# One accumulation instead of two: the other row half's carried products in a recurrent-attention kernel

## The chip, the cores and the metric

The kernel runs on one core of a Trainium2 chip. The core has a matrix engine (TensorE; PE in the rows below, with PEld for its weight loads), a vector engine (DVE), a scalar engine (ACT), a general engine (POOL) and a queue that issues transfers (SP). Matmul results land in eight accumulator banks of 128 rows by 512 words; only PE, DVE and ACT reach them. The metric is the device time of one execution in microseconds (us), lower is better.

## The reference

Two parts follow each other, over 4 sequences of 768 positions.

```python
# part 1, for 8 heads of 40: a gated outer-product memory
m_new = np.maximum(f[t] + m, i[t])
C = exp(f[t] + m - m_new) * C + exp(i[t] - m_new) * outer(v[t], k[t])
n = exp(f[t] + m - m_new) * n + exp(i[t] - m_new) * k[t]
y[t] = sigmoid(o[t]) * (C @ q[t]) / maximum(abs(n @ q[t]), 1.0)
# part 2, for 4 experts of 64 on x = y: causal softmax attention of each
# expert, of which the two with the largest gate logits are summed
out = sum over the two of w[e] * (softmax(causal(q_e @ k_e.T / 8)) @ v_e @ wo[e])
```

## The kernel before

Part 1 works through 24 chunks of 128 positions (4 sequences of 6; they are numbered 0 to 23 through all sequences here), each of two sub-chunks of 64 positions. A chunk's output is the sum of two products: the *intra* products (scores inside a sub-chunk times values) and the *carried* products (queries times the state that the sub-chunk begins with). The first four chunks take another way ("narrow"); the other 20 are what the change is about.

For these 20, TensorE is used as tiles of 64 rows by 64 columns. The 8 heads lie in two row halves, and two matmuls on different row halves run side by side if they write different banks. The intra products of head parity a come from row half a and go to bank `py[a]`. The carried products of heads 0 to 3 come from row half 0 and those of heads 4 to 7 from row half 1. So half of the carried products have the row half of the bank that they belong to, here called the *same half*, and the rest have the other one, the *cross* products. Before, the same half is added to `py` by the matmuls themselves, while the cross products go to two spare banks `pi`, are copied by ACT to a tile `pc`, and DVE adds `pc` to `py`. After that ACT takes the absolute value of each head's denominator (tile `two`), DVE reduces it (`den`), multiplies with the output gate and the reciprocal, and the result `xt` is turned by PE (matmuls `one<-cst,xt`) for part 2.

All matmul results are views of one ring of eight banks, called `one`. In the rows below `one<-nat,dm` are the intra products of a chunk, `one<-sts,qs` its carried products, `one<-kqs` the scores of the next chunk, `one<-nat,ks` the next chunk's state increments. Part 2's projections are `one<-xh,WH`, `one<-WH,xh` and the like, its scores `one<-KH,QH`, its transposes `one<-cst,A`, its mixing `one<-AT,V`. A trace counts each of these 4-byte matmuls twice (two passes).

The order of the work is written as strings of steps (`UNIT`: S is a chunk's output, I the scores of the next, C its increments, L a load, P its decay tables, X the transposes, and small letters are part 2). A planner (`Tape.plan`) records all instructions, keeps matmuls in groups, and sets each engine's order by costs that it assumes; it may take up to twelve groups ahead if the first one would wait. So an edit in one step can move instructions of every engine. All instructions are emitted at one line, L618.

Of the kernel before, what the change touches and what calls it, by code (L numbers as in the profile page):

```python
# [19 lines left out]
HALF = S // 2  # L20
D1 = D + 1
T = P // 2
# [47 lines left out]
    "f45 m43 s46 f46 r45 p7,1 r44 m44 r46 s47 f47 r47 m45 m46 m47 p7,0 p7,2"  # L70
)
FIRST = (
    "S0 I0 C0 L0 P0 q0 X0 S1 I1 C1 L1 P1 k0 v2 X1 S2 I2 C2 L2 P2 g q1 k1 X2"
)
UNIT = (
    "m0 S0 I0 C0 L0 v0 v1 X0 P0 f0 s0 f1 s1 S1 I1 C1 L1 m1 k0 q0 p0 p1 p2 X1 f2 s2 s3 f3 P1 S2 I2 C2 q1 "
    "k1 v2 g P2 f4 f5 s4 s5 L2 X2"
)
PENULT = (
# [556 lines left out]
def mlstm_moe_kernel(ctx, tc, kq, nat, ig, fg, wqkv, wo, const, out):  # L636
# [3 lines left out]
    nc = tape = Tape(tc.nc)  # L640
# [5 lines left out]
    def buf(tag, shape, dtype=F32):  # L646
        return View(Buf(rings[tag], shape, dtype))
# [67 lines left out]
    eG = keep("eG", [P, NPE * H], F32)  # L715
# [7 lines left out]
    def dm_from_pe(b, j):  # L723
        return b == 0 and j < NPE

    def narrow(b, j):

        return b * NCH + j < NARROW
# [392 lines left out]
        state[b] = sprev  # L1121
        p1st[(b, j, "i")] = (nt, qc, dm, sin)

    def carried(b, j, out, pairs, start=False, stop=False):

        _, qc, _, sin = p1st[(b, j, "i")]
        for g in range(2):
            for k, zas in enumerate(pairs):
                for sub in range(j == 0, 2):
                    for z, a in zas:  # L1130
                        nc.tensor.matmul(
                            out(z, a)[rows[sub], g * D1 : (g + 1) * D1],
                            qc[heads[z], 2 * g + a, rows[sub]],
                            sin[sub][heads[z], 2 * g + a, :],
                            start=start and g == k == 0,
                            stop=stop and g == 1 and zas is pairs[-1],
                        )

    def sums(b, j):

        nm = f"{b}_{j}"
        py = [one(f"py_{nm}_{a}") for a in range(2)]
        pe = dm_from_pe(b, j)
        nt, _, dm, _ = p1st[(b, j, "i")]
        tape.cut(True)
        for c in range(4):
            for sub in range(2):
                for r, p in zip(rows, py):
                    nc.tensor.matmul(
                        p[rows[sub], c * D1 : (c + 1) * D1],  # L1150
                        dm[r, c, sub, :],
                        nt[r, (sub * 4 + c) * D1 : (sub * 4 + c + 1) * D1],
                        start=c == 0,
                        stop=c == 3 and (pe or j == 0 and sub == 0),
                    )
        tape.cut()
        pyv = [p[:, : 4 * D1].rearrange("p (c d) -> p c d", d=D1) for p in py]
        if not pe:
            pi = [one(f"pi_{nm}_{z}") for z in range(2)]
            tape.cut(True)  # L1160
            carried(b, j, lambda z, a: pi[z], (((0, 1), (1, 0)),), True, True)
            carried(b, j, lambda z, a: py[a][:, 2 * z * D1 :], (((0, 0), (1, 1)),), stop=True)
            tape.cut()
            r = slice(T if j == 0 else 0, P)
            pc = buf("pc", [P, 2, 2 * D1], F32)
            for z in range(2):
                nc.scalar.activation(pc[r, z], pi[z][r, : 2 * D1], AF.Copy)
                y = py[1 - z][r, 2 * z * D1 : 2 * (z + 1) * D1]
                nc.vector.tensor_tensor(y, y, pc[r, z], op=ALU.add)
        else:  # L1170
            pi = [one(f"pi_{nm}_{z}") for z in range(2)]
            tape.cut(True)
            carried(b, j, lambda z, a: pi[z][:, 2 * a * D1 :], (((0, 0), (1, 0)), ((0, 1), (1, 1))), True, True)
            tape.cut()
            r = slice(T if j == 0 else 0, P)
            n = P - r.start
            pc = buf("facb", [P, 2, 2, 2, D1], F32)
            for z in range(2):
                nc.vector.tensor_tensor(
                    pc[r, z],  # L1180
                    pi[z][r, : 4 * D1].rearrange("p (a g d) -> p a g d", a=2, g=2),
                    eG[r, j * H + 4 * z : j * H + 4 * z + 4]
                    .rearrange("p (g a) -> p a g", g=2)[:, :, :, None]
                    .to_broadcast([n, 2, 2, D1]),
                    op=ALU.mult,
                )
            for a in range(2):
                y = py[a][r, : 4 * D1].rearrange("p (z g d) -> p z g d", z=2, g=2)
                nc.vector.tensor_tensor(y, y, pc[r, :, a], op=ALU.add)
        p1st.pop((b, j, "i"))  # L1190
        return pyv

    def p1_state(b, j):
        nt = p1st[(b, j, "i")][0]
        o_n = nt[:, 2 * NV + DM :] if narrow(b, j) else nt[:, NKV:NNAT]
        xf = buf("xt", [P, 3 * P], F32)
        eo = xf[:, 0:DM].rearrange("p (h d) -> p h d", d=D)
        nc.scalar.activation(xf[:, 0:DM], o_n, AF.Tanh, scale=0.5)
        if narrow(b, j):
            parts = [(sums_narrow(b, j), slice(0, H))]  # L1200
        else:
            parts = [(y, slice(a, H, 2)) for a, y in enumerate(sums(b, j))]
        den = buf("den", [P, H], F32)
        twos = two[(b * NCH + j) % len(two)]
        for y, hs in parts:
            nc.scalar.activation(twos[:, hs, 0], y[:, :, D], AF.Abs, scale=2.0)
        nc.vector.tensor_reduce(den, twos, axis=AX.X, op=ALU.max)
        dens = den[:, :, None].to_broadcast([P, H, D])
        if b * NCH + j < EX:
            for y, hs in parts:  # L1210
                nc.vector.scalar_tensor_tensor(y[:, :, 0:D], eo[:, hs], 1.0, y[:, :, 0:D], op0=ALU.add, op1=ALU.mult)
            nc.vector.reciprocal(den, den)
            for y, hs in parts:
                nc.vector.tensor_tensor(eo[:, hs], y[:, :, 0:D], dens[:, hs], op=ALU.mult)
        else:
            for y, hs in parts:
                nc.vector.scalar_tensor_tensor(eo[:, hs], eo[:, hs], 1.0, y[:, :, 0:D], op0=ALU.add, op1=ALU.mult)
            nc.vector.reciprocal(den, den)
            tape.either(eo, eo, dens, op=ALU.mult)
        nc.scalar.activation(xf[:, DM : 3 * P], xf[:, 2 * P : DM], AF.Copy)  # L1220
        p1st[(b, j, "x")] = xf
# [442 lines left out]
    def run(text, k):  # L1664

        for f in text.split():
            a = int(f[1:] or 0)
            n = 3 * k + SH + a
            if f[0] == "S" and 3 <= n - 1 < NC:
                p1_state(*chunks[n - 1])  # L1670
            elif f[0] == "I" and n < NC:
                p1_intra(*chunks[n])
            elif f[0] == "C" and n < NC:
# [91 lines left out]
```

## Time and profile before

| what | us |
|---|---|
| median of three runs | 292.54 |
| the three runs | 292.54, 294.46, 291.70 |
| span of the profiled execution | 291.4 |

The profiled execution is known by its span, from its first to its last instruction; that is 0.3 us under the fastest of the three runs and 1.1 us under their median. Times in the rows are us from the start of that span. A matmul's end is modelled, and matmuls overlap, so the distance between two starts tells more than one matmul's length.

### The profile page before, as it was taken

Reading aid. Unit: us, or ns where it says so; the run is one execution under the profiler, and the core shown is the slowest. Engines: PE = TensorE matmul, PEld = TensorE weight load, DVE = VectorE, ACT = ScalarE, POOL = GpSimd, SP = SyncE. Lnnn points to the kernel's source line nnn. Section 1 sums busy time; section 2 is a strip of 40 time slices with the busy share of each in tenths; the row PEclk is TensorE's granted clock in tenths of the full one; section 3 lists DMA queues with packets and bytes.
Section 4 is the critical chain, followed back from the end, with each engine's and each line's share of the span. In section 5 each row is a group of like instructions: output and inputs, shape, how many; then the busy total and the mean of one; then the engine's idle time right before and its main releaser. Section 6 shows DMA issues by size and latency. Waiting matters only on the chain.

```text
span 291.4 us, 12993 instructions
## 1 busy us (share of the span) xinstructions
PE 279.5 (96%) x5128; PEld 242.2 (83%) x5128; DVE 220.7 (76%) x852; ACT 213.8 (73%) x714; POOL 166.5 (57%) x284
## 2 busy tenths in 40 slices
PE   8988999869999999999999999999999999999994
PEld 3876898759889978799889978798989976987884
DVE  7679387847896897657886888577878895588983
ACT  8983459829895887657895887567876895597971
POOL 3678298858889556958587628955870341014000
PEclk9999999979999999999999999999999999999999
DMA  7989769983566455645453537625401000100101
GB/s 217 293 262 282 188 178 236 251 188 110 130 194 184 116 157 167 172 124 169 137 173 112 170 100 200 196 95 146 133 6 71 2 0 2 71 3 0 70 26 45
DMA packets 31580, 39.18 MB, mean 134 GB/s; under 512 B 2784, under 2 KB 25280, under 8 KB 31520
## 3 DMA queue, kind: packets, MB, share of 16 engines
q1 hardware_dynamic: 31472, 38.26, 45.9%
q8 instruction: 40, 0.66, 0.9%
q14 instruction: 20, 0.16, 0.2%
q10 hardware_dynamic: 48, 0.10, 0.1%
HBM read 34.22 MB, written 4.13 MB: 132 GB/s over the span
## 4 chain that ended last, share of the span: by engine, by line
PE 74%; DVE 8%; ACT 5%; issue 4%; DMA 4%; POOL 3%; SPq 1%; DVEq 0%; ACTq 0%; POOLq 0%
PE one L618 74%; DMA nat<-in_nat 4%; ACT dm L618 2%; DVE A L618 2%; POOL qs L618 1%; SPq L618 1%; DVE one L618 1%; DVE sts L618 1%; ACT A L618 1%; POOL yl L618 1%; ACT AT L618 1%; DVE dm L618 0%; DVE facb L618 0%; POOL xt L618 0%; DVE xt L618 0%
## 5 line engine op out<-in xcount | busy, mean ns | idle before, releaser
L618 ACT ACTIVATE A<-A,nmx 128x128 f32<-128x128 f32 (+5 forms) x96 | 64.0, 671 | 3.7 <-DVE nmx L618 3.5
L618 DVE CUSTOM_DVE_ANT_0 A<-one,maskw 128x384 f32<-128x384 f32 (+4 forms) x96 | 45.0, 495 | 0.4
L618 ACT ACTIVATE AT<-one 128x256 f32<-128x256 f32 (+3 forms) x96 | 35.5, 428 | 6.3 <-PE one L618 6.1
L618 PE MATMUL one<-AT,V 128*64 128x384 f32 (+2 forms) x360 | 39.8, 370 | 0.0
L618 PE MATMUL one<-xl,WH 128*128 128x384 f32 x96 | 33.2, 346 | 2.3 <-issue 2.3
L618 PE MATMUL one<-xh,WH 128*128 128x384 f32 x96 | 34.7, 361 | 0.5 <-DVE xt L618 0.5
L618 PEld LDWEIGHTS one<-AT,V 128*64 128x64 f32 x360 | 22.5, 137 | 14.9 <-issue 11.6
L618 POOL TENSOR_TENSOR qs<-kqs,eqs 112x512 f32<-112x512 f32 x20 | 26.2, 1311 | 10.8 <-PE one L618 10.5
L618 PE MATMUL one<-cst,A 64*128 64x64 f32 x672 | 31.6, 226 | 0.0
L618 PEld LDWEIGHTS one<-cst,A 64*128 64x128 f32 x672 | 27.5, 138 | 2.9 <-issue 0.6
L618 POOL TENSOR_TENSOR dm<-dm,cst 128x512 f32<-128x512 f32 x20 | 25.7, 1286 | 6.3 <-DMA dm<-gd 5.0
L618 PE MATMUL one<-KH,QH 64*128 64x384 f32 (+4 forms) x128 | 27.2, 375 | 0.0
L618 POOL TENSOR_TENSOR ks<-nat,dm 128x320 f32<-128x320 f32 x24 | 17.8, 743 | 14.5 <-ACT dm L618 6.9
L618 PE MATMUL one<-KL,QH 64*128 64x384 f32 (+4 forms) x128 | 23.9, 319 | 0.0
L618 PE MATMUL one<-KH,QL 64*128 64x384 f32 (+4 forms) x128 | 23.8, 319 | 0.0
L618 DVE COPY AT<-one 128x384 f32<-128x384 f32 (+3 forms) x48 | 21.0, 456 | 2.5 <-PE one L618 2.2
L618 PEld LDWEIGHTS one<-xh,WH 128*128 128x128 f32 x96 | 18.5, 193 | 4.6 <-issue 3.4
L618 ACT ACTIVATE xh<-one 128x192 fp32r<-128x192 f32 (+1 forms) x45 | 13.0, 335 | 12.3 <-PE one L618 12.2
L618 PE MATMUL one<-xh,WL 128*128 128x384 f32 x64 | 22.0, 343 | 0.0
L618 PE MATMUL one<-WH,xh 128*128 128x260 f32 x72 | 21.5, 301 | 0.0
L618 DVE TENSOR_TENSOR dm<-one,dm 128x256 f32<-128x256 f32 (+1 forms) x44 | 18.7, 440 | 3.3 <-POOL ks L618 3.1
L618 DVE CUSTOM_DVE_ANT_0 A<-one,maskw,nmx 128x320 f32<-128x320 f32 (+1 forms) x32 | 18.5, 579 | 2.8 <-DVE nmx L618 1.0
(143 smaller groups left out, 812.9 us busy)
## 6 DMA issues: line engine op xcount, KB each, us to landing
kqs<-in_kq SPq DMA_DIRECT2D x24, 448.0 KB, 5.6
nat<-in_nat SPq DMA_DIRECT2D x20, 484.0 KB, 5.7
dm<-gd SPq DMA_DIRECT2D x40, 128.0 KB, 3.7
eqs<-ge SPq DMA_DIRECT2D x40, 96.0 KB, 5.3
out<-ob SPq DMA_DIRECT2D x24, 160.0 KB, 1.9
nat<-in_nat SPq DMA_DIRECT2D x4, 320.0 KB, 6.4
A<-in_wqkv SPq DMA_DIRECT2D x3, 386.0 KB, 6.8
nat<-in_nat SPq DMA_DIRECT2D x8, 82.0 KB, 6.3
```

What stands on the lines that cost most here:

```text
L618: f(*[fix(x) for x in op.a], **{k: fix(v) for k, v in op.k.items()})
```

## The change

The cross products are no longer given banks of their own. `sums` now issues the intra products and the same half in one group and returns; a new step N (`p1_rest`), which stands behind I and C, issues the cross products into `py` itself and then the rest of the denominators. Between the two, ACT takes those denominators of `py[1]` that are complete already (the second half of its heads). With this the denominators take three ACT instructions instead of two. The copies to `pc`, the additions and the banks `pi` are left for chunk 23 alone, which has no next chunk. A branch for chunks that compute their decay table on PE, which no wide chunk took, goes as well.

```diff
 UNIT = (
-    "m0 S0 I0 C0 L0 v0 v1 X0 P0 f0 s0 f1 s1 S1 I1 C1 L1 m1 k0 q0 p0 p1 p2 X1 f2 s2 s3 f3 P1 S2 I2 C2 q1 "
+    "m0 S0 I0 C0 N0 L0 v0 v1 X0 P0 f0 s0 f1 s1 S1 I1 C1 N1 L1 m1 k0 q0 p0 p1 p2 X1 f2 s2 s3 f3 P1 S2 I2 C2 N2 q1 "
...
+        carried(b, j, lambda z, a: py[a][:, 2 * z * D1 :], ((0, 0), (1, 1)), stop=True)
         tape.cut()
...
+        if later:
+            return by_head(py)
+        pi = [one(f"pi_{nm}_{z}") for z in range(2)]
+        tape.cut(True)
+        carried(b, j, lambda z, a: pi[z], ((0, 1), (1, 0)), True, True)
+        tape.cut()
...
+        if not narrow(b, j) and later:
+            nc.scalar.activation(twos(b, j)[:, H // 2 + 1 :: 2, 0], parts[1][0][:, 2:4, D], AF.Abs, scale=2.0)
+            p1st[(b, j, "s")] = xf, parts
+            return
...
+    def p1_rest(b, j):
+
+        if (b, j, "s") not in p1st:
+            return
+        xf, parts = p1st.pop((b, j, "s"))
+        tape.cut(True)
+        carried(b, j, lambda z, a: parts[a][0][:, 2 * z : 2 * z + 2, :].rearrange("p c d -> p (c d)"), ((0, 1), (1, 0)), stop=True, skip_group_check=True)
+        tape.cut()
+        p1st.pop((b, j, "i"))
+        nc.scalar.activation(twos(b, j)[:, 0:H:2, 0], parts[0][0][:, :, D], AF.Abs, scale=2.0)
+        nc.scalar.activation(twos(b, j)[:, 1 : H // 2 : 2, 0], parts[1][0][:, 0:2, D], AF.Abs, scale=2.0)
+        finish(b, j, xf, parts)
...
-                p1_state(*chunks[n - 1])
+                p1_state(*chunks[n - 1], n < NC)
+            elif f[0] == "N" and 3 <= n - 1 < NC:
+                p1_rest(*chunks[n - 1])
```

On PE, at chunk 14 (about 140 us in the trace), the first two rows of each kind stand in this order before; the number behind `one` is the bank, and the first carried pair writes the spare banks 65 and 70, the second the banks 68 and 67 of the intra products:

```order
L618 MATMUL one_68<-nat_157,dm_82 64x41
L618 MATMUL one_67<-nat_157,dm_82 64x41
...
L618 MATMUL one_65<-sts_162,qs_85 64x41
L618 MATMUL one_70<-sts_162,qs_85 64x41
...
L618 MATMUL one_68<-sts_162,qs_85 64x41
L618 MATMUL one_67<-sts_162,qs_85 64x41
...
L618 MATMUL one_66<-kqs_148 64x64
L618 MATMUL one_64<-kqs_148 64x64
...
L618 MATMUL one_69<-nat_155,ks_154 64x41
L618 MATMUL one_63<-nat_155,ks_154 64x41
...
L618 MATMUL one_65<-WH_172,xh_91 128x260
```

And now, on the same engine at the same chunk:

```order
L618 MATMUL one_70<-nat_157,dm_82 64x41
L618 MATMUL one_64<-nat_157,dm_82 64x41
...
L618 MATMUL one_70<-sts_162,qs_85 64x41
L618 MATMUL one_64<-sts_162,qs_85 64x41
...
L618 MATMUL one_63<-kqs_148 64x64
L618 MATMUL one_65<-kqs_148 64x64
...
L618 MATMUL one_66<-nat_155,ks_154 64x41
L618 MATMUL one_67<-nat_155,ks_154 64x41
...
L618 MATMUL one_64<-sts_162,qs_85 64x41
L618 MATMUL one_70<-sts_162,qs_85 64x41
...
L618 MATMUL one_68<-WH_172,xh_91 128x260
```

Eight of the sixteen carried matmuls moved behind the next chunk's scores and increments and write the intra products' banks 64 and 70; the number of matmuls is the same.

On ACT, at chunk 14, the order before was (`A` is an exponential of part 2, `dm` that of a decay table, `xt<-nat` the output gate's tanh, `yh` a copy of part 2):

```order
L618 ACTIVATE A_77,zs_107<-A_77,nmx_129 128x384
L618 ACTIVATE pc_86<-one_65 128x82
L618 ACTIVATE pc_86<-one_70 128x82
L618 ACTIVATE A_76,zs_107<-A_76,nmx_128 128x256
L618 ACTIVATE two_164<-one_68 128x4
L618 ACTIVATE two_164<-one_67 128x4
L618 ACTIVATE dm_81<-dm_81 128x512
L618 ACTIVATE xt_88<-nat_155 128x320
L618 ACTIVATE yh_117<-R_140 128x384
```

And now:

```order
L618 ACTIVATE A_77,zs_107<-A_77,nmx_129 128x384
L618 ACTIVATE A_76,zs_107<-A_76,nmx_128 128x256
L618 ACTIVATE two_164<-one_64 128x2
L618 ACTIVATE dm_81<-dm_81 128x512
L618 ACTIVATE xt_88<-nat_155 128x320
L618 ACTIVATE two_164<-one_70 128x4
L618 ACTIVATE two_164<-one_64 128x2
L618 ACTIVATE yh_117<-R_140 128x384
```

The copies are gone, and the last denominators of the chunk moved behind one `dm` and one `xt<-nat`.

On SP, where chunks 8 to 10 are loaded (rows `kqs_148`, `eqs_152`, `dm_80` and `nat_155` are the loads of chunk 9, `dm_82` and `nat_157` those of chunk 8):

```order
 L618 DMA eqs_151<-ge 48x4x128 x2
 L618 DMA dm_82<-gd 64x4x128 x2
 L618 DMA nat_157<-in_nat 128x968
+L618 DMA dm_80<-gd 64x4x128 x2
+L618 DMA nat_155<-in_nat 128x968
 L618 DMA kqs_148<-in_kq 112x1024
 L618 DMA eqs_152<-ge 48x4x128 x2
-L618 DMA dm_80<-gd 64x4x128 x2
-L618 DMA nat_155<-in_nat 128x968
 L618 DMA kqs_149<-in_kq 112x1024
```

Two loads of chunk 9 moved ahead of its other two.

## Rows read from the trace of the kernel before

**Rows 1.** The page: span, busy time of each engine, the queue that fetches instructions

```profile
span 291.4 us, 12993 instructions
...
PE 279.5 (96%) x5128; PEld 242.2 (83%) x5128; DVE 220.7 (76%) x852; ACT 213.8 (73%) x714; POOL 166.5 (57%) x284
...
q8 instruction: 40, 0.66, 0.9%
```

**Rows 2.** Busy time by stretch: length, engines, granted clock, DMA share, GB/s

```profile
40.00:57.70 17.70, 16.45 (x457) 14.72 (x455) 14.10 (x64) 15.97 (x69) 15.35 (x20) 1.00 0.98 251
57.70:61.50 3.80, 0.93 (x23) 0.69 (x16) 3.07 (x14) 1.65 (x7) 3.18 (x6) 1.00 1.14 229
61.50:66.00 4.50, 4.50 (x27) 4.15 (x27) 0.56 (x1) 1.38 (x3) 1.52 (x5) 0.62 0.52 139
66.00:270.00 204.00, 203.52 (x3878) 178.22 (x3877) 159.17 (x636) 156.18 (x521) 121.69 (x211) 1.00 0.38 112
```

**Rows 3.** Groups of instructions by form: count, busy us and mean ns, idle before

```profile
L618 PE MATMUL one<-sts,qs 40*64 40x41 f32 x592 | 13.7, 227 | 0.6 <-DVE xl L618 0.6
...
L618 DVE TENSOR_TENSOR one<-one,pc 128x82 f32<-128x82 f32 x34 | 7.1, 244 | 2.8 <-ACT pc L618 2.5
...
L618 ACT ACTIVATE pc<-one 128x82 f32<-128x82 f32 x34 | 6.2, 234 | 3.2 <-PE one L618 3.0
...
L618 ACT ACTIVATE two<-one 128x4 f32<-128x4 f32 x40 | 5.6, 175 | 0.5 <-DVE one L618 0.4
```

**Rows 4.** Timeline at chunk 14: start, us, engine, instruction, idle before it

```profile
139.55 0.68 PE L618 MATMUL one<-nat,dm 64*64 64x41 f32 x32
...
140.04 0.66 PE L618 MATMUL one<-sts,qs 40*64 40x41 f32 x32
140.21 0.19 ACT L618 ACTIVATION_READ_ACCUMULATOR A<-A,nmx 128x1 f32 x1
...
140.50 0.67 PE L618 MATMUL one<-kqs 40*64 40x64 f32 x32
140.57 0.37 ACT L618 ACTIVATE pc<-one 128x82 f32<-128x82 f32 x2 [0.17 <-PE one L618]
140.82 0.51 ACT L618 ACTIVATE A<-A,nmx 128x256 f32<-128x256 f32 x1
...
141.00 0.84 PE L618 MATMUL one<-nat,ks 64*64 64x41 f32 x32
141.22 0.20 ACT L618 ACTIVATION_READ_ACCUMULATOR A<-A,nmx 128x1 f32 x1
...
141.58 0.24 ACT L618 ACTIVATE two<-one 128x4 f32<-128x4 f32 x2 [0.16 <-DVE one L618]
141.72 0.63 ACT L618 ACTIVATE dm<-dm 128x512 f32<-128x512 f32 x1
...
142.26 0.46 ACT L618 ACTIVATE xt<-nat 128x320 f32<-128x320 f32 x1
...
143.66 0.26 ACT L618 ACTIVATE xt<-xt 128x64 f32<-128x64 f32 x1 [0.30 <-DVE xt L618]
...
143.89 0.40 PE L618 MATMUL one<-cst,xt 64*128 64x64 f32 x6
```

**Rows 5.** Timeline of PE around its longest idle time

```profile
58.76 0.33 PE L618 MATMUL one<-xh,WL 128*128 128x384 f32 x1
61.44 0.33 PE L618 MATMUL one<-xl,WH 128*128 128x384 f32 x1 [2.34 <-issue]
...
64.83 0.52 PE L618 MATMUL one<-xh,WH 128*128 128x384 f32 x1
65.15 0.44 PE L618 MATMUL one<-xl,WH 128*128 128x384 f32 x1
```

**Rows 6.** DMA queues from 57.7 to 61.5 us: packets, MB, share of 16 engines

```profile
q1 hardware_dynamic: 1045, 0.85, 112.4%
q8 instruction: 1, 0.02, 2.1%
```

More of the change, by code (lines that the diff above doesn't have):

```diff
@@ L72 @@
 FIRST = (
-    "S0 I0 C0 L0 P0 q0 X0 S1 I1 C1 L1 P1 k0 v2 X1 S2 I2 C2 L2 P2 g q1 k1 X2"
+    "S0 I0 C0 N0 L0 P0 q0 X0 S1 I1 C1 N1 L1 P1 k0 v2 X1 S2 I2 C2 N2 L2 P2 g q1 k1 X2"
 )
 UNIT = (
-    "m0 S0 I0 C0 L0 v0 v1 X0 P0 f0 s0 f1 s1 S1 I1 C1 L1 m1 k0 q0 p0 p1 p2 X1 f2 s2 s3 f3 P1 S2 I2 C2 q1 "
+    "m0 S0 I0 C0 N0 L0 v0 v1 X0 P0 f0 s0 f1 s1 S1 I1 C1 N1 L1 m1 k0 q0 p0 p1 p2 X1 f2 s2 s3 f3 P1 S2 I2 C2 N2 q1 "
     "k1 v2 g P2 f4 f5 s4 s5 L2 X2"
@@ L1122, in p1_inc, with carried, sums @@
         p1st[(b, j, "i")] = (nt, qc, dm, sin)
-    def carried(b, j, out, pairs, start=False, stop=False):
+    def carried(b, j, out, zas, start=False, stop=False, **k):
         _, qc, _, sin = p1st[(b, j, "i")]
         for g in range(2):
[L1128 to L1139, printed above, removed]
+            for sub in range(j == 0, 2):
+                for z, a in zas:
+                    nc.tensor.matmul(
+                        out(z, a)[rows[sub], g * D1 : (g + 1) * D1],
+                        qc[heads[z], 2 * g + a, rows[sub]],
+                        sin[sub][heads[z], 2 * g + a, :],
+                        start=start and g == 0,
+                        stop=stop and g == 1,
+                        **k,
+                    )
+    def sums(b, j, later):
         nm = f"{b}_{j}"
         py = [one(f"py_{nm}_{a}") for a in range(2)]
-        pe = dm_from_pe(b, j)
         nt, _, dm, _ = p1st[(b, j, "i")]
@@ L1153, in sums @@
                         start=c == 0,
-                        stop=c == 3 and (pe or j == 0 and sub == 0),
+                        stop=c == 3 and j == 0 and sub == 0,
                     )
+        carried(b, j, lambda z, a: py[a][:, 2 * z * D1 :], ((0, 0), (1, 1)), stop=True)
         tape.cut()
[L1157 to L1189, printed above, removed]
@@ L1190, in sums @@
-        p1st.pop((b, j, "i"))
-        return pyv
-    def p1_state(b, j):
+        if later:
[4 more added lines that the diff above has]
+        tape.cut()
+        r = slice(T if j == 0 else 0, P)
+        pc = buf("pc", [P, 2, 2 * D1], F32)
+        for z in range(2):
+            nc.scalar.activation(pc[r, z], pi[z][r, : 2 * D1], AF.Copy)
+            y = py[1 - z][r, 2 * z * D1 : 2 * (z + 1) * D1]
+            nc.vector.tensor_tensor(y, y, pc[r, z], op=ALU.add)
@@ L1194, in p1_state, with by_head, twos @@
+        p1st.pop((b, j, "i"))
+        return by_head(py)
+    def by_head(py):
+        return [
+            (p[:, : 4 * D1].rearrange("p (c d) -> p c d", d=D1), slice(a, H, 2)) for a, p in enumerate(py)
+        ]
+    def twos(b, j):
+        return two[(b * NCH + j) % len(two)]
+    def p1_state(b, j, later=False):
         nt = p1st[(b, j, "i")][0]
@@ L1196, in p1_state @@
         xf = buf("xt", [P, 3 * P], F32)
-        eo = xf[:, 0:DM].rearrange("p (h d) -> p h d", d=D)
         nc.scalar.activation(xf[:, 0:DM], o_n, AF.Tanh, scale=0.5)
@@ L1201, in p1_state, with finish @@
         else:
-            parts = [(y, slice(a, H, 2)) for a, y in enumerate(sums(b, j))]
+            parts = sums(b, j, later)
+        if not narrow(b, j) and later:
+            nc.scalar.activation(twos(b, j)[:, H // 2 + 1 :: 2, 0], parts[1][0][:, 2:4, D], AF.Abs, scale=2.0)
+            p1st[(b, j, "s")] = xf, parts
+            return
+        for y, hs in parts:
+            nc.scalar.activation(twos(b, j)[:, hs, 0], y[:, :, D], AF.Abs, scale=2.0)
+        finish(b, j, xf, parts)
[9 more added lines that the diff above has]
+        nc.scalar.activation(twos(b, j)[:, 1 : H // 2 : 2, 0], parts[1][0][:, 0:2, D], AF.Abs, scale=2.0)
+        finish(b, j, xf, parts)
+    def finish(b, j, xf, parts):
+        eo = xf[:, 0:DM].rearrange("p (h d) -> p h d", d=D)
         den = buf("den", [P, H], F32)
[L1204 to L1207, printed above, removed]
+        nc.vector.tensor_reduce(den, twos(b, j), axis=AX.X, op=ALU.max)
         dens = den[:, :, None].to_broadcast([P, H, D])
```

## Prediction

> **What bounds the kernel now.** The page comes first: PE is busy 96% of the span, DVE 76%, ACT 73% [rows 1]. The table by stretch says where that holds [rows 2]. From 66 to 270 us PE is busy 203.52 of 204.00 us at the full granted clock, while DVE has 159.17 and ACT 156.18. So in 70% of the kernel only 0.48 us of PE's time waits for anybody, and work taken from DVE or ACT there is worth at most that. The stretch before is different: from 40 to 57.7 us PE idles 17.70 - 16.45 = 1.25 us, ACT is at 15.97 of 17.70, and the loads keep the DMA engines full (0.98). Then PE stands still from 58.76 to 61.44 us, of which 2.34 us are idle, with a matmul behind it that waits for no semaphore [rows 5], and after that it runs at the lower of its two clock levels for a while: granted 0.62 on average over 4.5 us, starts 0.32 us apart [rows 2, 5].
>
> The timeline of chunk 14 shows the piece that is edited [rows 4]. The starts on PE are 139.55 (intra), 140.04 (carried), 140.50 (next scores), 141.00 (next increments): 0.46 to 0.50 us for each 32 matmuls, and nothing in between. ACT waits 0.17 us for PE before the copies, DVE waits for ACT, and PE waits for neither.
>
> **What is taken away.** Each of 19 chunks loses two copies of 234 ns on ACT and two additions of 244 ns on DVE [rows 3], and gains a third denominator instruction of up to 175 ns. ACT gets 2 x 234 - 175 = 293 ns per chunk, 5.6 us in all; DVE 488 ns, 9.3 us in all. Of these, 16 chunks (7 to 22) lie after 66 us beside a PE that is full: worth 0 there, up to the 0.48 us. PE keeps every matmul. The spare banks return two of eight for about a microsecond per chunk, while `py` is held longer, through the next scores and increments; a wait for a bank would be PE idle time, and after 66 us that is inside the same 0.48 us. I take back half of it, -0.2 us.
>
> **What is added on PE.** The carried products split in two groups, with one more change of group per chunk. Bounds: 0, since the scores start at 140.50 while the carried products' record runs to 140.70, so a change of group costs no emptying [rows 4]; above, one matmul's length of 227 ns [rows 3], if PE had to run empty before the cross products, 19 x 0.227 = 4.3 us. I take 0, since all four changes in rows 4 are of that kind.
>
> In front of the cross products there is a new wait: PE waits for ACT's early denominators, because these read the bank that PE writes next. Behind it on PE stands everything, so it counts in full. Worked out at chunk 14: the exponential before the copies ends at 140.21 + 0.19 = 140.40; now another one of 128x256 stands ahead of the early denominators (the order shows it), which took from 140.82 to 141.42, so it ends at 141.00 and the denominators at 141.00 + 0.175 = 141.18. PE reaches the cross products at 139.55 + 0.49 + 0.23 + 0.50 + 0.50 = 141.27. So 0.1 us to spare: price 0. In most other chunks the order puts the early denominators just where the copies stood, and ACT stood ready for these: it waited 3.0 us for PE before them [rows 3].
>
> The Trainium skill, TensorEngine Tiling (Array Packing), section "Restrictions and Gotchas", says that different row tiles may not use one accumulator bank at the same time and that software must keep them apart. It speaks against putting the cross products into the other half's bank at all. The 1.0 us of scores and increments between them [rows 4] keeps them apart at no price; if the array had to be emptied instead, the sum would be the upper bound just given, 296.6 us.
>
> **What is moved.** The denominators come later. Before, they ended at 141.58 + 0.24 = 141.82. Now PE ends the cross products at about 141.27 + 0.23 + 0.23 = 141.7, but on ACT a `dm` and a tanh stand ahead of the last two; at their distances in rows 4 (0.54 and 0.36 us) these two start at 141.18 + 0.90 = 142.1 and end at 142.3, 0.5 us later than before. From there to the finished `xt` it took 143.66 + 0.26 - 141.82 = 2.1 us, and PE began the transposes at 143.89, with no slack. So the transposes of chunk 14 may wait up to 0.5 us; below, 0, because DVE has lost two additions and may run its part of the 2.1 us sooner. Chunks 8 and 20 stand alike in the order, at 11 and 17 the transposes are put behind other matmuls, and in the two other thirds of the chunks more of part 2 stands ahead of X. So 3 x 0 to 0.5 us: I take 0.25 each, since both effects are sure and of like size, +0.7 us.
>
> **The stretch from 40 to 66 us.** Here chunks 4 to 6 are edited, ACT gets 0.9 us of its 15.97 back, and PE's 1.25 us of waits may shrink: 0 to -1.25, I take -0.7. The pause at 58.76 us is the largest single item, and its cause must be named. 40 packets of 0.66 MB in all, 16.5 KB each, run on a queue of their own marked as instructions [rows 1]; one of them falls into the pause, beside a load queue that takes 112% of 16 engines [rows 6]. So I read it as PE out of instructions, because a fetch stood behind loads. Then the pause ends when the fetch lands, whatever PE saved before, and a part of the 0.7 us is lost in it. The order moves two loads of chunk 9 ahead of two others, the same bytes in the same few microseconds, so I take the pause as unchanged: 0, with a gain of all of it or a loss as the ends, below.
>
> The Trainium skill, Runtime: NRT & Kernel Launch, section "Instruction fetch mechanics", says that instructions come in blocks of 256 (16 KiB) over the engine's own DMA queue while it executes, and that this is mostly hidden. The packets of 16.5 KB agree with the block; the pause does not agree with "hidden". By that rule the pause would be something else and no order of loads would move it: the first rival below would have no chance, and the forecast would stay.
>
> **Sum.** -0.2 + 0 + 0 + 0.7 - 0.7 = -0.2 us against the profiled 291.4 us, which is 1.1 us under the median of the runs. I lay the same difference on the median: 292.54 - 0.2 = 292.3 us. A measurement of this kernel tells about 1% (2.9 us) from no change: its own runs lie 0.9% apart.
>
> **Rivals.**
> 1. The pause goes. Loads and matmuls around 50 to 58 us stand in another order, and a fetch that gets ahead of the loads costs nothing. For it: the pause is one event of one packet. Against it: the queue is full before and after. Price: 2.34 us of idle time and 4.5 x (1 - 0.62) = 1.7 us at the lower clock, 4.0 us: 288.3 us; with all of the 1.25 us before it, 287.0.
> 2. Slower, by late denominators. Place: ACT, the last two denominators of the chunks whose transposes come first after S (8, 11, 14, 17, 20, and 5 before 66 us). It decides from the point where `xt` is ready later than 143.89 in chunk 14's terms, and there is no slack. If not DVE's additions but ACT's order sets that chain, and a copy of part 2 or an exponential stands ahead as well, each is late by 0.5 to 1.0 us: 6 x 0.75 = 4.5 us, of which I had 0.7: 296.1 us.
> 3. The pause grows. The moved loads are 128 + 484 KB; at 229 GB/s [rows 2] a fetch behind them comes 2.7 us later: 295.0 us.
> 4. The change doesn't take off what it says: had the copies been on PE's path, PE would show waits for DVE at `one`; it shows none in rows 4, so this is the forecast itself.
>
> **Chances.** Forecast 0.60, rival 1 0.24, rival 2 0.12, rival 3 0.04. The forecast's own range is 290.5 to 294.5 us (its two open terms, and half a per cent of scatter). The range for 8 in 10 reaches into rival 1, down to its lower half, and to rival 3 above: 287.2 to 295.3. Faster by over 1% is rival 1, 0.24; slower by over 1% is rival 2 and the worse half of rival 3 and of an unlucky forecast, 0.15; the rest, 0.61, is within 1%.
>
> **What would show it.** The table by stretch: PE again full from 66 to 270 us, ACT lower by some 5 us and DVE by some 8 us there, at the same length. At chunk 14: scores 0.23 us earlier after the intra products, cross products right behind the increments without idle time, denominators about 0.5 us later, and PE idle before `one<-cst,xt` by 0 to 0.5 us. Around 58 us: the pause of some 2.3 us with no semaphore, and the clock row under 1 behind it. The forecast is wrong if the pause is gone or longer, if PE shows idle time before the cross products that ACT ends, or if waits for `xt` add to several microseconds.

## The result, and the profile after

The changed kernel takes 296.59 us (median of 11 runs, 294.70 to 297.45) where the kernel before took 294.46 us in the runs beside it (11 runs, 291.70 to 296.73): ratio 1.0092, 95% interval 1.0065 to 1.0118. By this ratio, which is taken over the fast runs alone and so isn't that of the two medians (1.007), it is slower by 2.7 us: inside 1%, but the interval doesn't reach 1. The forecast was 292.3 us, no change.

The page of the changed kernel, in the rows that answer to [rows 1]:

```profile
span 294.8 us, 12917 instructions
...
PE 280.2 (95%) x5128; PEld 242.0 (82%) x5128; DVE 214.6 (73%) x814; ACT 209.9 (71%) x695; POOL 166.4 (56%) x284
...
q8 instruction: 40, 0.66, 0.9%
```

ACT has lost 3.9 us of work and DVE 6.1, and the span grew by 3.4 us. The table by stretch, which answers to [rows 2], says where:

```profile
40.00:57.70 17.70, 14.10 (x369) 12.91 (x368) 10.77 (x43) 12.31 (x53) 13.61 (x18) 0.98 0.89 231
57.70:61.50 3.80, 3.80 (x94) 3.40 (x92) 2.49 (x15) 3.06 (x15) 2.41 (x3) 0.66 1.07 234
61.50:66.00 4.50, 1.82 (x13) 1.50 (x9) 2.88 (x14) 1.87 (x7) 3.17 (x4) 1.00 1.00 240
66.00:270.00 204.00, 202.94 (x3855) 177.47 (x3857) 152.16 (x597) 151.63 (x501) 121.22 (x215) 0.99 0.38 112
```

From 40 to 57.7 us PE idles 3.60 us (1.25 before), from 61.5 to 66 us 2.68 us. From 66 us on it is full again but for 1.06 us, of which the first 0.74 are the end of a stop. The waits of PE, longest first (what was waited for, sum, times, longest), give these stops a name that is no engine ("issue" means that PE waited for nothing that the trace shows):

```profile
PE one L618 <- issue: 7.0, 3, 3.4
PE one L618 <- POOL ks L618: 1.2, 2, 0.8
```

Three stops of 7.0 us in all. Before there was one under this name, of 2.34 us [rows 5]. PE's timeline around them (start, length, instruction, idle time before it):

```profile
52.65 0.34 PE L618 MATMUL one<-sts,qs 40*64 40x41 f32 x5
55.94 0.54 PE L618 MATMUL one<-sts,qs 40*64 40x41 f32 x19 [2.94 <-issue]
...
62.81 0.34 PE L618 MATMUL one<-xl,WH 128*128 128x384 f32 x1
62.99 0.34 PE L618 MATMUL one<-xh,WH 128*128 128x384 f32 x1
66.74 0.44 PE L618 MATMUL one<-xh,WL 128*128 128x384 f32 x1 [3.42 <-issue]
67.02 0.46 PE L618 MATMUL one<-xl,WH 128*128 128x384 f32 x1
67.28 0.52 PE L618 MATMUL one<-xh,WH 128*128 128x384 f32 x1
67.60 0.52 PE L618 MATMUL one<-xh,WL 128*128 128x384 f32 x1
```

The second stop stands in the middle of one chunk's products, and the third between two matmuls of the same group, of which the second reads nothing that this group had not read before (there was an `xh,WL` at 62.29 us). Both look like the pause of [rows 5]. Behind the third, starts are 0.26 to 0.32 us apart instead of 0.17 to 0.18: the lower clock. From 40 to 75 us as a whole the granted clock was 0.95 before and is 0.90 now:

```profile
40.00:75.00 35.00, 30.88 (x693) 28.09 (x692) 25.17 (x111) 26.80 (x106) 27.94 (x40) 0.95 0.83 208
40.00:75.00 35.00, 27.98 (x644) 25.52 (x643) 20.95 (x92) 22.40 (x94) 22.82 (x33) 0.90 0.74 183
```

In place of the chain of waits, four landmarks of both traces say what each stretch of the program gained or lost. They are starts of intra products:

| stretch | before | after | difference |
|---|---|---|---|
| start to chunk 4 | 44.68 | 45.53 | +0.85 |
| chunk 4 to chunk 7 | 22.13 | 25.71 | +3.58 |
| chunk 7 to chunk 22 | 156.72 | 155.29 | -1.43 |
| chunk 22 to the end | 67.87 | 68.27 | +0.40 |

The first line is scatter: nothing is edited there, and the profiles below reach chunk 4 between 44.7 and 46.8 us with either kernel (those with padding aside). The last line is not: from chunk 22 to the end the ten profiles with the new way of chunk 23, where the cross products now come ahead of the intra products, take 68.1 to 68.3 us, and the eight others 67.7 to 67.9. PE has no idle time between chunk 23 and its last matmul in either kernel, and where these 0.4 us go wasn't found. So the changed chunks of the long stretch got faster, and the three at 45 to 71 us lost more than that.

Chunk 14, the answer to [rows 4]:

```profile
143.94 0.68 PE L618 MATMUL one<-nat,dm 64*64 64x41 f32 x32
...
144.43 0.42 PE L618 MATMUL one<-sts,qs 40*64 40x41 f32 x16
...
144.66 0.67 PE L618 MATMUL one<-kqs 40*64 40x64 f32 x32
...
145.15 0.63 PE L618 MATMUL one<-nat,ks 64*64 64x41 f32 x32
145.19 0.16 ACT L618 ACTIVATE two<-one 128x2 f32<-128x2 f32 x1
...
145.59 0.42 PE L618 MATMUL one<-sts,qs 40*64 40x41 f32 x16
...
146.12 0.23 ACT L618 ACTIVATE two<-one 128x4 f32<-128x4 f32 x2
...
147.95 0.26 ACT L618 ACTIVATE xt<-xt 128x64 f32<-128x64 f32 x1 [0.36 <-POOL xt L618]
148.05 0.47 PE L618 MATMUL one<-cst,A 64*128 64x64 f32 x8
...
148.35 0.36 PE L618 MATMUL one<-cst,xt 64*128 64x64 f32 x6
```

The cross products start 0.44 us behind the increments, with no idle time, and the early denominators had ended at 145.35, 0.24 us before PE needed their bank. Counted from the chunk's first matmul, the denominators end at 2.41 us (2.27 before), `xt` is done at 4.27 (4.37 before), and PE does other transposes first and waits for nothing.

### The profile page after: what moved, and what is told of

It reads as the page before. It is cut to its first block, busy times and chain, and to the rows that moved or that the text cites. A ratio compares the mean times of both kernels' runs of the same rounds, so it can differ in the third digit from the quotient of the medians.

```text
span 294.8 us, 12917 instructions
## 1 busy us (share of the span) xinstructions
PE 280.2 (95%) x5128; PEld 242.0 (82%) x5128; DVE 214.6 (73%) x814; ACT 209.9 (71%) x695; POOL 166.4 (56%) x284
## 4 chain that ended last, share of the span: by engine, by line
PE 80%; DVE 6%; ACT 5%; issue 5%; POOL 3%; DVEq 0%; ACTq 0%; POOLq 0%
PE one L618 80%; ACT A L618 2%; DVE A L618 2%; ACT dm L618 1%; DVE AT L618 1%; DVE sts L618 1%; POOL yl L618 1%; POOL AT L618 1%; ACT facb L618 1%; DVE one L618 1%; POOL xt L618 0%; DVE WL L618 0%; DVE facb L618 0%; POOL cd L618 0%; ACT yh L618 0%
## 5 line engine op out<-in xcount | busy, mean ns | idle before, releaser
L618 ACT ACTIVATE AT<-one 128x256 f32<-128x256 f32 (+3 forms) x94 | 34.2, 421 | 7.9 <-PE one L618 7.5
L618 POOL TENSOR_TENSOR dm<-dm,cst 128x512 f32<-128x512 f32 x20 | 25.7, 1284 | 2.4 <-DMA dm<-gd 1.4
L618 DVE COPY AT<-one 128x384 f32<-128x384 f32 (+3 forms) x50 | 22.4, 469 | 6.2 <-PE one L618 6.1
L618 POOL TENSOR_TENSOR ks<-nat,dm 128x320 f32<-128x320 f32 x24 | 17.8, 740 | 16.0 <-ACT dm L618 10.7
L618 DVE TENSOR_TENSOR dm<-one,dm 128x256 f32<-128x256 f32 (+1 forms) x44 | 18.1, 443 | 8.1 <-POOL ks L618 4.0
L618 POOL TENSOR_SCALAR fac<-zs 128x6 f32<-128x6 f32 x14 | 3.3, 238 | 35.0 <-ACT A L618 18.3
```

What stands on the lines that cost most here:

```text
L618: f(*[fix(x) for x in op.a], **{k: fix(v) for k, v in op.k.items()})
```

## The experiments

Three theories. **A**: PE stops where its fetched instructions end, and the change's new order around 45 to 66 us makes these stops longer; in itself it gains. **B**: the later denominators and the split of the carried products cost time in every chunk. **C**: PE waits at these places for a transfer or an engine whose event the trace doesn't show.

One count stands behind A. Number all of PE's instructions in a trace (matmuls, weight loads and some 140 waits and drains of its queue) in order of start. Before, PE stopped after 1729 (0.68 us) and 1985 (2.34 us). After, it stopped after 1473, 1729 and 1985 (0.66, 2.94, 3.42 us). All these are 193 behind a multiple of 256, and each stop ended 1.3 to 1.6 us after a packet of the instruction queue had ended. The stop after 1729 stood among the 1.25 us of waits in the prediction, since the trace puts it down to DVE:

```profile
53.74 0.27 PE L618 MATMUL one<-cst,xt 64*128 64x64 f32 x1
54.70 0.39 PE L618 MATMUL one<-cst,xt 64*128 64x64 f32 x5 [0.68 <-DVE sts L618]
```

In the texts below "number" is this count.

### Half of the change

The change in the later chunks alone, and in the first three alone, by one condition; the other chunks work as before, and up to chunk 7's products PE's order is that of the kernel before (`steady_only`) or of the changed one (`ramp_only`):

```diff
-                p1_state(*chunks[n - 1], n < NC)
+                p1_state(*chunks[n - 1], n < NC and n - 1 >= 7)   # steady_only; ramp_only: n - 1 < 7
```

> The change in chunks 7 to 22 alone; chunks 4 to 6 keep the spare banks, copies and additions, and up to chunk 7 every engine has the order of the kernel before. Theory A (the loss is made by the order around 45 to 66 us, where PE runs out of fetched instructions; the change itself gains 1.3 us between chunk 8 and chunk 23): idle time with no semaphore stands where it stood before, 3 us in all at the matmuls and weight loads number 1729 and 1985; ratio 0.993 to 1.000. Theory B (later denominators and the split of the carried products cost time in every chunk): ratio 1.005 to 1.01, as for the whole change, and PE idle time before the transposes.

> The change in chunks 4 to 6 alone; up to chunk 7 every engine has the order of the changed kernel, after that chunks 7 to 22 work as before. Theory A: 7 us of idle time with no semaphore at numbers 1473, 1729 and 1985 (0.7, 2.9 and 3.4 us in the profile of the changed kernel), and without the 1.3 us of gain behind it; ratio 1.010 to 1.018. Theory B: three chunks of nineteen are edited, so ratio 0.998 to 1.003.

Measured: the later chunks alone 0.9996 (0.9952 to 1.0039), the first three alone 1.0080 (1.0035 to 1.0124). In the profiles the stops are 0.74 and 1.50 us after 1729 and 1985 in the first, and 0.38, 2.66 and 0.79 us after 1473, 1729 and 1985 in the second. The second is under the range that A gave (1.010 to 1.018), since its stops were 3.8 us and not 7. So the loss is in chunks 4 to 6. B is out: 16 edited chunks cost nothing that the runs can tell, and three cost about all of it.

### Where the packets end

More instructions at the beginning move the ends of the 256-blocks to other matmuls, with every order as it was. First 64 tiny matmuls were put among the ones that warm PE up:

```diff
+                for _ in range(64):
+                    f(o[:T, 0:T], w[:, :T], w[:, :T], start=True, stop=True)
```

> The changed kernel with 64 matmuls of 64 columns more among the first ones, which multiply zeros while PE waits for its first data; every engine's order is otherwise the same. They are 128 matmuls and weight loads, half of the 256 that a packet of the instruction queue holds. Theory A (PE stops where the fetched instructions end): the idle time without a semaphore stands again at numbers 193 behind a multiple of 256, counted with the added ones, so 128 earlier in the program, at other matmuls than in the changed kernel; its length changes by up to some us either way, ratio to the kernel before 0.99 to 1.015. Theory C (PE waits there for some transfer or engine whose event the trace does not show): it stands at the same matmuls as in the changed kernel (numbers 1601, 1857 and 2113 with the added ones), with 7 us in all; ratio 1.007 to 1.012.

> The kernel before with the same 64 added matmuls. Theory A: the idle time of 0.7 and 2.3 us at numbers 1729 and 1985 moves 128 earlier in the program and stands at numbers 193 behind a multiple of 256 again; its length may go up or down; ratio 0.985 to 1.015. Theory C: it stays at the same matmuls (1857 and 2113 with the added ones), 3 us in all; ratio 0.998 to 1.003.

This pair doesn't decide between A and C. The operand was 4 bytes wide, so each matmul went in two passes and 256 instructions were added, a whole block. The padded changed kernel stopped after 1729, 1985 and 2241, and the padded kernel before after 1985 (1.24 us) and 2241 (0.1 us, with starts 0.64 us apart): the same matmuls, as A and C both say. And the added matmuls took 13.8 us: ratios 1.0452 (1.0367 to 1.0538) and 1.0469 (1.0403 to 1.0534). The second pair cuts the 2-byte warm-up matmuls that are there, so that their columns stay the same:

```diff
+        n = SPLIT if self.seen > 1 else 2 * SPLIT      # SPLIT = 4
+            for c in range(0, 4 * P, 4 * P // n):
+                f(o[:, c : c + 4 * P // n], w, w[:, : 4 * P // n], **k)
```

> The changed kernel with its 20 first matmuls of 512 columns, which multiply zeros while PE waits for data, cut into 84 of 128 or 64 columns: the same columns, but 128 matmuls and weight loads more, half of the 256 in a packet of the instruction queue; all other orders are unchanged, and the start isn't to be later by more than 0.5 us. (The padded kernels before failed at this: their matmuls went in two passes, so 256 were added, a whole packet, and cost 14 us.) Theory A: the idle time without a semaphore is again at numbers that lie 193 behind a multiple of 256, so at other matmuls, 128 earlier in the program; length 2 to 9 us in all, ratio to the kernel before 0.985 to 1.015. Theory C: at the same matmuls as in the changed kernel (numbers 1601, 1857, 2113), 7 us in all, ratio 1.006 to 1.012.

> The kernel before with the same cut. Theory A: idle time at numbers 193 behind a multiple of 256, other matmuls than before, ratio 0.985 to 1.015. Theory C: at numbers 1857 and 2113, 3 us in all, ratio 0.998 to 1.002.

Measured: 1.0058 (1.0014 to 1.0102) and 1.0183 (1.0110 to 1.0257). The stops of the changed kernel now come after 1985, 2497, 3265, 4545, 5057, 5825 and 7105, and those of the kernel before after 1729, 3265, 4545, 5057, 5825 and 7105. Every one is 193 behind a multiple of 256 again, at matmuls where neither kernel ever stopped, as A says and C can't. PE's timeline of the changed kernel with the cut shows three of them:

```profile
81.35 0.54 PE L618 MATMUL one<-AT,V 128*64 128x384 f32 x1
83.42 0.54 PE L618 MATMUL one<-AT,V 128*64 128x384 f32 x2 [1.54 <-issue]
...
116.19 0.26 PE L618 MATMUL one<-nat,ks 64*64 64x41 f32 x2
117.75 0.44 PE L618 MATMUL one<-nat,ks 64*64 64x41 f32 x16 [1.31 <-issue]
...
148.25 0.63 PE L618 MATMUL one<-nat,ks 64*64 64x41 f32 x32
149.75 0.44 PE L618 MATMUL one<-sts,qs 40*64 40x41 f32 x16 [0.87 <-ACT A L618]
```

The last is put down to ACT, yet it ended 1.44 us behind a packet, as the others did (1.29 to 1.52 us): a wait's name can hide a fetch. What the cut took from the early stops it gave back later. The changed kernel went from chunk 4 to chunk 7 in 16.96 us instead of 25.71, and from chunk 8 to chunk 22 in 152.29 instead of 145.74. With this cut the changed kernel is the faster of the two.

### Loads in front of the fetch

Fewer loads under way: ahead of the loads of chunks 8 and 9, SP issues a transfer of 4 bytes that reads the tile which the chunk before loaded last, and so waits for it.

```diff
+            self.nc.sync.dma_start(self.gate[0:1, k : k + 1], self.nats[c - 1][0:1, 0:1])
```

> The changed kernel, with the loads of chunk 8 issued only when chunk 7's largest load has landed, and those of chunk 9 when chunk 8's has (a transfer of 4 bytes that reads the landed tile stands ahead of them on SP). Fewer loads are under way at once around 50 to 64 us. Theory A (the fetch waits behind loads): the packets of the instruction queue start sooner; idle time at number 1985 falls from 3.4 to under 1.5 us and at 1729 from 2.9 to under 2.5; ratio to the kernel before 0.985 to 1.002. Theory C (PE waits there for a load or an engine): the loads come 3 to 6 us later, so the idle time stays or grows; ratio 1.008 or more.

> The kernel before with the same two holds. Theory A: idle time at number 1985 falls from 2.3 to under 0.8 us; ratio 0.985 to 0.998. Theory C: ratio 1.000 or more.

And more of them: a copy of 0.5 MB between the loads of chunks 8 and 9 that nobody reads.

```diff
+            self.nc.sync.dma_start(self.gate, self.nats[c - 1])
```

> The kernel before with one transfer more on SP between the loads of chunks 8 and 9 (at about 52.7 us): the 0.5 MB of chunk 8's largest load again, copied to a scratch place in device memory that nobody reads. Theory A (the fetch stands behind loads): the packet of the instruction queue that started at 58.66 starts 1.5 to 4 us later, and the idle time at number 1985 grows from 2.3 to 4 to 6.5 us; ratio 1.003 to 1.015. If PE's stop has nothing to do with the loads: it stays at 2 to 2.5 us; ratio 0.998 to 1.002.

Measured: 0.9986 (0.9950 to 1.0022), 0.9968 (0.9927 to 1.0008), 1.0056 (1.0013 to 1.0098). With the holds, the changed kernel's packets that had started at 53.49 and 64.11 us started at 51.95 and 60.00, and its stops went from 0.66, 2.94 and 3.42 to 1.00, 1.30 and 0.60 us. PE's own progress moves these times too, so count from the start of number 1536 or 1792, 193 instructions before the end of the block: the packets started 2.58 and 5.73 us behind these in the changed kernel (1.78 and 5.58 in the repeat below) and 0.86 and 3.68 with the holds; in the kernel before 1.78 and 3.27, with the holds 0.41 and 2.53. C had the holds make the changed kernel slower, and its loss is gone with them, so C is out and loads do delay the fetch. The extra copy doesn't add to this: its packet started at 60.89 instead of 58.66 us, but PE came to 1792 later by as much (3.13 us from there to the packet). Two more expectations missed. In the kernel before, the hold left 1.37 us of the 2.34 where under 0.8 was expected (`steady_only`, with the same order and no hold, has 1.50). With the extra copy the stop after 1985 was not 4 to 6.5 us but this:

```profile
62.68 0.52 PE L618 MATMUL one<-xh,WL 128*128 128x384 f32 x1
63.70 0.48 PE L618 MATMUL one<-xl,WH 128*128 128x384 f32 x1 [0.50 <-issue]
```

PE got there at 62.68 instead of 58.76 us: the stop after 1729 had grown to 1.45 us, and behind it PE ran at the lower clock, as the row of 57.7 to 66 us has it (granted 0.50):

```profile
57.70:66.00 8.30, 7.80 (x117) 6.98 (x113) 5.03 (x23) 3.85 (x19) 4.64 (x8) 0.50 0.97 239
```

So the extra copy's 1.0056 is no proof of a fetch behind loads. The holds weren't free either: the changed kernel with them needed 148.89 us from chunk 8 to chunk 22, with new waits for late data at 80 to 83 us (`xt` 0.96 us, `sts` 0.47 us), while POOL waited 1.7 us for the load of a `dm`.

### The loads or PE's order

The change moved loads of chunks 7 and 9 on SP, and instructions of all engines. Here each kernel gets the load order of the other for these two chunks, its other engines unchanged:

```diff
+            moved = [op for op in order if mine(op, late)]
+            order = [op for op in order if op not in moved]
...
+            order[k:k] = moved
```

> The changed kernel with the loads of chunks 7 and 9 on SP in the order of the kernel before; the other engines keep the order of the changed kernel. If the order of the loads makes the longer stops: stops at 1729 and 1985 of about 0.7 and 2.3 us, ratio 0.993 to 1.000. If the order on PE makes them (chunk 6's sums right behind chunk 5's use up the fetched instructions sooner): the stop at 1729 stays at 1.3 us or more, ratio 1.003 to 1.010.

> The kernel before with the loads of chunks 7 and 9 in the order of the changed kernel, the other engines as before. If the order of the loads makes the longer stops: ratio 1.007 to 1.015. If PE's order does: 0.998 to 1.004.

> The changed kernel once more, unedited, beside these on the same chip. Theory A: stops at numbers 1473, 1729 and 1985 again, at the same matmuls, 4 to 8 us in all (their lengths depend on when loads and packets meet); ratio 1.005 to 1.012.

Measured: 1.0038 (1.0007 to 1.0068), 0.9980 (0.9943 to 1.0017), and the unedited changed kernel beside them 1.0086 (1.0052 to 1.0121). The new load order does no harm to the kernel before, and with the old one the changed kernel is still slower than the kernel before. So the order on the engines is needed for the loss. Whether the load order adds to it there is not shown: 1.0038 is about half of the loss, but its interval overlaps that of 1.0086. Neither expectation on the stops came true for the changed kernel with the old load order: they were 1.03 us after 1729, none after 1985, 0.89 after 2241, and 0.58 and 0.68 us at 82 and 88 us. The repeat stopped after the same three numbers, 0.32, 2.12 and 1.75 us long: the places are the program's, the lengths are not. Its stops are 2.8 us shorter than in the first profile, and its clock is lower:

```profile
40.00:75.00 35.00, 30.81 (x653) 28.20 (x651) 21.80 (x96) 23.89 (x96) 24.13 (x37) 0.85 0.78 192
```

### A better place for the ends of the packets

Two edits. One keeps the cut and puts 64 tiny matmuls behind chunk 7's products, so that from there on the blocks end where they did at first. The other cuts only the first eight warm-up matmuls, 48 instructions more, a number chosen from the two traces: with it few runs of 256 after 70 us are short.

```diff
+        if self.align and op.n >= self.align and op.call == "matmul" and op.k.get("start"):
+            for _ in range(64):
+                f(o[:T, 0:16], w[:T, :T], w[:T, 0:16], start=True, stop=True)
...
+        if self.seen > 8:
+            return f
```

> The changed kernel with the cut first matmuls (128 more matmuls and weight loads, which took most of the idle time out of 40 to 66 us), and 64 matmuls of 64 rows by 16 columns more behind chunk 7's products, so that from there on the ends of the 256-packets fall on the same matmuls as in the changed kernel, where they cost nothing. Theory A: no idle time at numbers 193 behind a multiple of 256 after 70 us (the cut alone had five, of 1.0 to 2.1 us); the 64 added matmuls cost 1 to 4 us; ratio to the kernel before 0.975 to 0.995. If the ends of the packets don't set these stops: five stops of 1 to 2 us as with the cut alone, ratio 1.005 or more.

> The kernel before with the same two edits. Theory A: ratio 0.978 to 0.998, and slower than the changed kernel with these edits by 1 to 3 us, which is what the change itself is then worth (1.4 us from chunk 7 to chunk 22, up to 0.8 before). Theory B (the change costs time in every chunk): faster than the changed kernel with these edits.

> The changed kernel with only the first eight of its first matmuls cut into four: 48 matmuls and weight loads more. Theory A: idle time without a semaphore only at numbers 193 behind a multiple of 256, so 48 earlier in the program; after 70 us hardly any, since there the 256 that end at such numbers take 2.7 us or more in the changed kernel's trace; between 45 and 66 us 2 to 7 us; ratio to the kernel before 0.98 to 1.01.

> The kernel before with the first eight of its first matmuls cut into four, as in the changed kernel that came out at 0.9951: 48 matmuls and weight loads more. Whether that gain came from the change or from where the packets end: if from the change, ratio 0.999 to 1.005 here; if from the packets' ends alone, 0.990 to 0.998. In the trace of before the 256 that end at the new places between 45 and 66 us take 2.7 to 7.8 us, the shortest at 49 us, so a stop of 0.5 to 2 us there is expected, and fewer than 1 us of stops after 70 us.

The first came out at 1.0086 (1.0047 to 1.0125) for the changed kernel and 1.0005 (0.9968 to 1.0042) for the kernel before, against the expectation and in B's sense. The stops after 70 us are gone, as A said, but the added matmuls ran into one themselves, 2.81 us in the changed kernel and 1.16 in the other, and PE's clock was low behind it (starts 0.32 us apart):

```profile
64.87 0.74 PE L626 MATMUL one<-wz 64*64 64x16 bf16 x19
68.43 1.75 PE L626 MATMUL one<-wz 64*64 64x16 bf16 x43 [2.81 <-issue]
...
71.23 0.52 PE L618 MATMUL one<-xh,WH 128*128 128x384 f32 x1
71.55 0.52 PE L618 MATMUL one<-xh,WL 128*128 128x384 f32 x1
```

B has its loss in every chunk, and that isn't so here: in the two profiles the changed kernel is faster from chunk 8 to chunk 22 (146.1 against 147.3 us) and slower only from chunk 7 to chunk 8 (16.0 against 14.4), where the added matmuls stand. But the spans of these profiles differ by 1.0 us and the medians of the runs by 2.6, and the rest is not explained.

The second made the changed kernel 293.0 us, 0.9951 (0.9914 to 0.9989): faster than both kernels without it. Its waits for nothing known:

```profile
PE one L618 <- issue: 2.4, 2, 1.6
```

The same 48 instructions made the kernel before slower, 1.0128 (1.0079 to 1.0176), outside both ranges expected for it, with a stop of 3.69 us after 1729 and one of 1.40 us after 7105. So that gain is neither the change's nor the shift's, but how the two meet.

All of it in one table: the stops between 40 and 71 us in the one profile that each kernel has, the granted clock from 40 to 75 us, two stretches of that profile, and the ratio of the runs to the kernel before. A profile is one execution and the ratio is over many, and stops differ between executions (the repeat), so the columns need not go together line by line.

| kernel | stops, us | clock | chunk 4 to 7 | chunk 8 to 22 | ratio |
|---|---|---|---|---|---|
| before | 3.0 | 0.95 | 22.1 | 147.1 | 1 |
| after | 7.0 | 0.90 | 25.7 | 145.7 | 1.0092 |
| after, again | 4.2 | 0.85 | 24.3 | 146.1 | 1.0086 |
| steady_only | 2.2 | 1.00 | 19.7 | 145.6 | 0.9996 |
| ramp_only | 3.8 | 0.90 | 22.8 | 146.5 | 1.0080 |
| after_split, before_split | 1.4, 0.5 | 1.00, 1.00 | 17.0, 17.8 | 152.3, 155.5 | 1.0058, 1.0183 |
| after_hold, before_hold | 2.9, 1.7 | 0.95, 0.95 | 20.3, 20.7 | 148.9, 146.8 | 0.9986, 0.9968 |
| before_extra | 2.2 | 0.85 | 23.5 | 146.9 | 1.0056 |
| after_loads, before_loads | 1.9, 1.2 | 0.90, 0.90 | 21.3, 20.8 | 147.2, 147.2 | 1.0038, 0.9980 |
| after_realign, before_realign | 2.8, 1.7 | 0.95, 0.95 | 17.7, 17.9 | 146.1, 147.3 | 1.0086, 1.0005 |
| after_shift48, before_shift48 | 2.4, 3.7 | 0.90, 0.95 | 21.0, 22.4 | 147.6, 148.4 | 0.9951, 1.0128 |

## Why the prediction was wrong

**The step that failed** is "so I take the pause as unchanged: 0". The prediction had named the cause rightly (PE out of instructions, the fetch behind loads) and then held its length for fixed, because the same bytes are loaded in the same few microseconds. The stops grew from 3.0 to 7.0 us, and the lower clock behind them cost more as well: 5.5 x (1 - 0.69) = 1.7 us from 56 to 61.5 us and 5.3 x (1 - 0.68) = 1.7 us from 66.7 to 72 us, where the kernel before has 5.1 x (1 - 0.67) = 1.7 us once. What the length depends on is two times, and the change moved both. When does the packet start? At 53.49 and 64.11 us, where it had been 52.05 and 58.66. And when does PE reach the end of what it has? For 1729 at 52.77 instead of 53.74 us, because chunk 6's intra products now stand right behind chunk 5's. This second time is the steadier one. From number 1536 to the stop PE needs 1.85 or 1.86 us in each profile in which the block ends at that matmul in the new order, and 3.47 or 3.48 in the old one, so 1.6 us less to hide a fetch in. The stop after 1729 is longer in the three profiles with the new order and no edit of the loads (2.94, 2.12, 2.66 us) than in the two with the old one (0.68, 0.74), and the padded pair agrees (2.66 and 1.24). The holds show it, too: with the packet at 51.95 us a stop of 1.30 us was left. The stop after 1985 is less certain: 3.42 us, but 1.75 in the repeat and 0.79 in `ramp_only`, where the kernel before has 2.34 and `steady_only` 1.50.

Rival 3, the pause grows, was the case. Its price, 295.0 us, lies close to the measured 292.54 x 1.0092 = 295.2, but by luck: it had one fetch wait behind 612 KB of moved loads, while two stops grew, and the load order alone does nothing (0.9980). The sum was short as well: two `dm` of 128 KB moved, not one, so 740 KB, 3.2 us and 295.5 us, and loads of chunk 7 had moved besides. It got a chance of 0.04, since the pause was looked at as one event; had the count of instructions been made on the trace of before, it would have shown the 0.68 us at 53.74 us as a second stop at the same place of a block, and that PE was on the edge twice.

**The gain of 0.7 us from 40 to 66 us** was taken from these 1.25 us of idle time. 0.68 of them were that stop, which no relief of ACT shortens. What engines had caused did go: the changed kernel has no wait like those of 0.56 and 0.53 us that ended at 45.9 and 58.5 us before.

**The late denominators** were mis-sized with the wrong sign: +0.7 us for three transposes, none of which waited. The denominators end 0.14 us later, not 0.5. The early ones ended at 1.41 us from the chunk's start instead of the 1.63 worked out, since ACT started its instructions about 0.1 us before the record of the one ahead ended (the exponential at 144.69 behind 144.60 + 0.20, the denominators at 145.19 behind 145.09 + 0.20), where the sum put them one after the other. From the last denominators to the finished `xt` it took 1.86 us instead of 2.10, and the order has other transposes ahead of `xt`'s.

**The change by itself** seems to gain. In the profiles that have no stop and no wait for loads between chunk 8 and chunk 22, that stretch takes 145.64 to 146.07 us with the change (four profiles, mean 145.9) and 146.47 to 147.29 without (six, mean 147.0): 1.1 us, where the sum had a loss of 0.5; the 0.4 us behind chunk 22 leave 0.7 of it. The runs can't confirm so little (steady_only: 0.9996, 0.9952 to 1.0039), and the changed kernel with 48 instructions more, with 147.63 us, is outside its group for 0.7 us of idle time and something that wasn't found. Most of the 1.1 us stand inside the chunks' own products. In ten chunks of this stretch the 128 matmuls from the intra products to the last of the block follow one another, and these ten blocks take 20.1 to 20.4 us together in the four profiles and 20.7 to 21.3 in the six: 2.01 us nearly everywhere with the change, but 2.13 to 2.20 without it at chunks 9 and 15 and 2.13 to 2.54 at chunk 21. In the profile of before PE waits 0.21 us there for DVE in the middle of the scores. That these are waits for a bank, which the two returned banks end, fits but was not tested; the sum had 0.2 us for it.

**What held**: the cross products cost no emptying of the array, PE doesn't wait for the early denominators, the scores come 0.23 us sooner after the intra products, and from 66 to 270 us ACT lost 4.6 us and DVE 7.0 with PE full as before.

The Trainium skill, Runtime: NRT & Kernel Launch, section "Instruction fetch mechanics", has blocks of 256 instructions and a fetch that is mostly hidden. The blocks agree with every stop here. "Hidden" holds for most of the 40 packets of these kernels (PE stopped at two of them before and at three after) and fails where loads are dense or the instructions short.

## What to carry to other kernels

Before costing an edit in a stage where PE stops for nothing the profile shows, count PE's instructions up to each stop: if the counts leave the same remainder when divided by 256 (193 here), it is most likely the fetch, and any edit that reorders instructions or loads there changes its length by microseconds that have nothing to do with the edit's own work. Judge such an edit with the blocks at several places (a few instructions more at the start). Over the four places that the block ends had here, it was slower at two (1.0092 as written; 1.0086 against 1.0005 with the cut and 64 matmuls) and faster at two (1.0058 against 1.0183 with the cut; 0.9951 against 1.0128 with 48 instructions). And a stop can cost as much again in the lower clock behind it: 35 us at 0.85 to 1.00 are 0 to 5 us.

## What the runs showed of the hardware

- In the 18 profiles taken here PE waits 42 times between 40 and 270 us for nothing that the trace names, and all 42 waits end at a number 193 behind a multiple of 256. PE went on mostly 1.3 to 1.7 us after the end of a packet that itself took 0.9 to 1.7 us.
- A stop needs no crowd of loads. A chunk's products are 256 such instructions in 2.0 us (64 for each 0.5 us in [rows 4]), while in the 42 stops it took 2.4 to 3.1 us from the start of the packet to PE's next matmul. Where a block's end falls among such products PE outran the fetch (after_split: 0.74 to 1.54 us, five times), with the DMA engines 32 to 75% busy from the instruction 193 ahead of the block's end to the restart. At 147.32 us the packet started only 0.04 us behind that instruction, and PE still stopped for 0.87 us. Three chunks of the long stretch are 1280 instructions, five blocks, so a bad place comes back with every three chunks: after_split and before_split both stopped after 3265, 4545, 5825 and 7105.
- With loads dense, a packet of 16.5 KB came late: in the changed kernel the one of 64.11 us started 5.7 us after number 1792 (5.6 in the repeat), and in the same kernel with the holds 3.7 us after it.
